# Seven products in place of eight for more of a linear attention's tiles, with the matrix's summed parts kept in memory

## The chip, the cores and the metric

The kernel runs on one core of one Trainium2 chip. The metric is the device time of one launch in microseconds, as the median of several runs; the profile is that of one more execution. Five engines matter: TensorE (PE, with its weight loads as PEld), VectorE (DVE), ScalarE (ACT), GpSimd (POOL) and SyncE (SP, which here only issues DMAs).

## The reference

A block of 2048 tokens of width 512 gets, in parallel, a linear attention with 32 heads of 16 and an MLP of 1376 hidden units with squared relu. All is float32.

```
xn  = layernorm(x)
q, k, v = split(xn @ wqkv)            # 512 x 1536
pq, pk  = phi(q), phi(k)              # phi(t) = (t > 0 ? t + 1 : exp(t)) + 1e-6
kv  = sum over tokens of pk^T v       # per head
z   = sum over tokens of pk
att = (pq @ kv) / (pq . z + 1e-6)     # per head
mlp = relu(xn @ w1 + b1)^2 @ w2 + b2
out = x + att @ wo + mlp
```

## The kernel before

**Number format and products.** Each float32 operand is held as a high and a low part (`split`: ScalarE copies to the high part, VectorE subtracts it to get the low part, called the rest), and each product is three matmuls, high by high, high by low, low by high (`PASSES`, L127). Moving operands are 512 columns wide, or 256 in the seven products.

**Order of the work.** All order is written by hand: each engine runs its instructions in the order in which the code issues them. First the kernel normalises, projects the keys and sums keys by tokens, for all 16 tiles of 128 tokens (to about 100 us). Then `kv`, block by block, is multiplied into `wo`: the result is one 512x512 matrix M (`matrix`, L948), so that attention is `q' @ M`, where q' is phi(q) divided by its denominator.

Then come two passes, n = 0 and 1, of two blocks each (a block is four tiles, 512 tokens): blocks t1 = 3 and t2 = 2 in pass 0, blocks 1 and 0 in pass 1. A pass starts with rounds p = 0 to 7 (L1171). In a round the columns `fa`, `fb` of the first weights are multiplied with both blocks at once, by seven products in place of eight (Strassen's scheme in Winograd's form). "w" rounds make hidden units of the MLP, "q" rounds queries; the order is q, w, q, w, w, w, w, and round 7 only finishes round 6. From round 4 on a round is on TensorE: A A11 and B A12 (12 matmuls), C S1 (6), the A22 product of the round before into its own bank (6), an MLP sum (12), A S2 (6), C S4 (6), a second MLP sum (12), A S3 (6).

Around that stand, in the code's order, these instructions of the other engines:

- L1184, VectorE, start of the round: reads the bank of the round before, ahead of the A22 product which goes on in that bank. Behind it stand on ScalarE a relu (L1190) and the copy of bank A (L1206).
- L1210, VectorE: adds bank B to that copy; then a relu of it (L1212).
- `hidden_2` (L457): square and high part on ScalarE, low part `s` on VectorE, once for each half of the hidden units; the MLP sums read `s`.
- `chunk_split`, `chunk_sums`, `last_split`: the next round's weights and their sums.
- L1311, VectorE: reads bank C after C S4; the next round's C S1 starts that bank anew. Then a relu (L1317).

**Steps.** The queries' way from raw q to q' is a list of steps per 128 columns (`steps_of`, L421): phi (two halves on ScalarE, L417 and L418, the last part on VectorE, L419), `weighted` (ScalarE, pz, L433), `sums` (VectorE, L438 and L439), `quotients` (L444 to L446), `divide` (L449) and, for block t1, `into_parts`. How many steps stand at which of a round's nine places says the table `AT`, for the part behind the rounds `AE`. A call of `step` takes the next of t1's list, or of t2's when t1's is empty.

**Attention.** `add_attention` (L517) adds one tile the plain way, 12 matmuls of 128x512. `Seven` (L972) does pairs of tiles r, r + 2 by seven products: it sums the four quarters of q' in place (`sums_o`), splits those sums into `so` (`parts_o`, with highs and lows), and has the same for M: sums (`sums_m`), and splits into `mt`. `run` is one product of 6 matmuls of 128x256, `into` adds a bank into the residual `res` (VectorE, L1036). In before, block 3 and block 2 are done the plain way, block 1 wholly by sevens, and block 0 by sevens for tiles 0 and 2 only. M goes raw to memory in pass 0 (`md`, L962), comes back in round 6 of pass 1, and VectorE and ScalarE sum and split it there. `matrix_parts` (L964) splits M itself for the plain way, in rounds 3 (one part), 4 (one) and 5 (two).

**Places shared in turn.** `mt` takes the place of the columns `xs0`, `so` that of `xs1`; raw M stands in the two places x0 and x1, which the residual's loads (`load_res`, L1134) take next. `add_bias` (L1143) adds b2 to the residual by accumulating DMAs on POOL.

## Time and profile before

| | |
|---|---|
| median of 3 runs (lowest, highest) | 408.36 us (408.32, 408.89) |
| the profiled execution: its time | 408.15 us |
| its span on the core | 406.4 us |
| mean granted clock of TensorE | 0.999 |
| matmuls | 1993 |

The span runs from the first to the last event of the core; the profiled execution's time holds 1.75 us more around it. In the rows of the profile an instruction stands with its start, its duration, engine, line, operation, and `out<-in` with the shape; in square brackets is the idle time of its engine before it and what ended it. Matmuls overlap: what one costs is the distance to the next one's start, not its duration. In the table of stages a row gives the stretch, its length, for each engine the busy time and the number of instructions, the granted clock, the share of the DMA engines and GB/s.

### The profile page before, as it was taken

How to read it: one execution, taken by the hardware profiler on the slowest of the kernel's cores; microseconds unless marked ns; L12 is line 12 of the kernel's file. 1: busy time of each engine (PE TensorE's matmuls, PEld its weight loads, DVE VectorE, ACT ScalarE, POOL GpSimd, SP SyncE). 2: the span in 40 equal slices, each digit the busy share in tenths (PEclk: the TensorE clock that was granted, in tenths of full speed). 3: DMA queues.
4: the chain of work that ended last, by engine and by line, in shares of the span. 5: the costliest groups of instructions: out<-in, count | busy, mean ns of one | idle time of the engine just before them, and what ended most of it. 6: DMA issues, size and time to landing. Idle time of an engine off the chain costs nothing.

```text
span 406.4 us, 5813 instructions
## 1 busy us (share of the span) xinstructions
PE 401.5 (99%) x1993; PEld 333.1 (82%) x1993; DVE 326.7 (80%) x598; ACT 274.0 (67%) x478; POOL 49.7 (12%) x81
## 2 busy tenths in 40 slices
PE   8999999999999999999999999999999999999996
PEld 7788888888788888888878888888888888888885
DVE  5886667587898999988349997567989688999885
ACT  5677777556888788886818751677587859848440
POOL 5443333220000000030000300000000200000300
PEclk9999999999999999999999999999999999999999
DMA  5856657910563231381564912412221856015612
GB/s 213 278 168 223 208 158 205 257 29 0 130 184 80 77 103 27 105 214 19 202 232 131 209 33 101 118 53 52 52 79 32 229 103 232 2 52 202 110 26 103
DMA packets 47550, 51.10 MB, mean 126 GB/s; under 512 B 8417, under 2 KB 31201, under 8 KB 47138
## 3 DMA queue, kind: packets, MB, share of 16 engines
q1 hardware_dynamic: 45138, 46.55, 37.0%
q0 software_dynamic: 2304, 4.20, 6.4%
q8 instruction: 15, 0.25, 0.2%
q14 instruction: 13, 0.11, 0.1%
q10 hardware_dynamic: 80, 0.00, 0.0%
HBM read 38.81 MB, written 10.75 MB: 122 GB/s over the span
## 4 chain that ended last, share of the span: by engine, by line
PE 97%; DMA 1%; DVE 1%; ACT 0%; issue 0%
PE acc L133 33%; PE b L497 33%; PE pk L378 11%; PE kx L398 11%; PE acc L508 2%; PE acc L1028 2%; PE pz L133 1%; PE x L1028 1%; DMA x<-in_A_x_dram 1%; PE b L133 1%; PE pz0b L133 1%; PE xh L1028 1%; PE y L1028 0%; PE acc L515 0%; PE pt L310 0%; DVE st L236 0%
## 5 line engine op out<-in xcount | busy, mean ns | idle before, releaser
L133 PE MATMUL acc<-w2r,s 128*128 128x512 f32 x477 | 113.0, 390 | 0.0
L133 PEld LDWEIGHTS acc<-w2r,s 128*128 128x128 f32 x477 | 89.2, 188 | 19.1 <-issue 0.7
L497 PE MATMUL b<-T,aop 128*128 128x512 f32 x336 | 83.5, 389 | 0.0
L497 PEld LDWEIGHTS b<-T,aop 128*128 128x128 f32 x336 | 63.0, 188 | 13.9 <-ACT t L114 0.8
L1147 POOL DMA_DIRECT2D res<-in_B_b_dram x16 | 14.4, 1042 | 277.8 <-DVE dt L439 91.0
L398 PE MATMUL kx<-pk,tok 128*128 128x512 f32 x192 | 46.0, 389 | 0.0
L398 PEld LDWEIGHTS kx<-pk,tok 128*128 128x128 f32 x192 | 36.0, 188 | 7.6 <-ACT pk L114 0.2
L497 PE MATMUL b<-xs0h,aop 128*128 128x512 f32 x112 | 36.9, 390 | 0.0
L114 ACT ACTIVATE aop<-S 128x512 fp32r<-128x512 f32 x28 | 17.5, 624 | 12.5 <-DVE S L735 12.5
L359 POOL TENSOR_TENSOR tok<-xp,tok 128x512 fp32r<-128x512 f32 x15 | 20.2, 1344 | 39.7 <-ACT tok L114 39.7
L497 PEld LDWEIGHTS b<-xs0h,aop 128*128 128x128 f32 x112 | 21.0, 188 | 4.4
L125 DVE TENSOR_TENSOR w2r<-r,w2r 128x512 fp32r<-128x512 f32 (+2 forms) x35 | 23.7, 681 | 0.5 <-ACT w2r L114 0.4
L114 ACT ACTIVATE w2r<-r 128x512 fp32r<-128x512 f32 x32 | 19.6, 619 | 6.4 <-PE acc L133 5.5
L122 DVE TENSOR_TENSOR aop<-S,aop 128x512 fp32r<-128x512 f32 x28 | 19.2, 687 | 4.8 <-ACT aop L114 4.4
L497 PE MATMUL b<-xs0l,aop 128*128 128x512 f32 x56 | 21.8, 389 | 0.0
L133 PE MATMUL acc<-mh,aTsr 128*128 128x512 f32 x64 | 20.7, 389 | 0.0
L122 DVE TENSOR_TENSOR s<-c,s 128x512 fp32r<-128x512 f32 x20 | 13.5, 688 | 8.7 <-ACT s L114 8.6
L497 PE MATMUL b<-xs1h,aop 128*128 128x512 f32 x56 | 19.5, 389 | 0.0
L114 ACT ACTIVATE T<-Tf 128x512 fp32r<-128x512 f32 x16 | 9.5, 624 | 14.4 <-DVE Tf L678 14.3
L114 ACT ACTIVATE c<-b 128x512 f32<-128x512 f32 x28 | 16.4, 587 | 2.6 <-PE b L497 2.4
L369 ACT ACTIVATE k<-pk 128x512 f32<-128x512 f32 x16 | 9.4, 590 | 9.9 <-PE pk L378 9.8
L114 ACT ACTIVATE pk<-k 128x512 fp32r<-128x512 f32 x16 | 10.1, 631 | 8.6 <-DVE k L373 8.5
(259 smaller groups left out, 828.3 us busy)
## 6 DMA issues: line engine op xcount, KB each, us to landing
r<-in_B_w_dram SPq DMA_DIRECT2D x49, 256.0 KB, 3.5
res<-in_A_x_dram SPq DMA_DIRECT2D x8, 512.0 KB, 4.7
res<-in_B_b_dram POOLq DMA_DIRECT2D x16, 256.0 KB, 5.8
out_dram<-res SPq DMA_DIRECT2D x15, 256.0 KB, 2.2
via<-xp SPq DMA_DIRECT2D x5, 512.0 KB, 2.8
xg<-via SPq DMA_DIRECT2D x20, 128.0 KB, 2.8
xTd<-t SPq DMA_DIRECT2D x8, 256.0 KB, 4.1
x<-in_A_x_dram SPq DMA_DIRECT2D x4, 512.0 KB, 4.1
```

Of the source, the lines that this page charges most:

```text
L114: nc.scalar.activation(o, i, AF.Copy, bias=bias)
L122: ENG[el].tensor_tensor(out=l, in0=src, in1=f32(h), op=OP.subtract)
L125: nc.vector.tensor_tensor(out=l, in0=src, in1=f32(h), op=OP.subtract)
L133: nc.tensor.matmul(ps, lhsT=a[u], rhs=b[v], start=first and n == 0, stop=last and n == 2)
L359: ENG[el].tensor_tensor(out=l, in0=src, in1=f32(h), op=OP.subtract)
L369: nc.scalar.activation(p, ps, AF.Relu, scale=-1.0)
L378: nc.tensor.matmul(ps, lhsT=cols(i)[u][:, j, slot(i)], rhs=w[v][:, j, :], start=first and n == 0, stop=last and n == len(steps) - 1)
L398: nc.tensor.matmul(kxp[c], lhsT=tok[i][:, u, c * P:(c + 1) * P], rhs=pk[i][:, v], start=i == 0 and (u, v) == first, stop=i == NT - 1 and ( ...
L497: nc.tensor.matmul(ps, lhsT=a[u][:, j * P:(j + 1) * P], rhs=b[v][:, j, :], start=first and j == 0 and n == 0, stop=last and j == 1 and n == 2,
L508: nc.tensor.matmul(ps, lhsT=s[u][:, k * P:(k + 1) * P], rhs=w2s[NF - 1][u][:, a:z], start=first and u == 0, stop=stop and u == 1)
L1028: nc.tensor.matmul(ps, lhsT=a, rhs=b, start=first and i == 0 and n == 0, stop=False, skip_group_check=True)
L1147: nc.gpsimd.dma_start(r[:, i], b2[None, :].partition_broadcast(P), accum_op=OP.add)
```

## The change

- In pass 0, tiles 0 and 2 of block 3 (the pass's first block) get attention by seven products, tiles 1 and 3 the plain way (`seven_half`). Block 3's q' is summed and split for that in round 6 and behind the rounds; block 2 stays plain.
- In pass 1, all four tiles of block 0 go by seven products; the MLP sum of one chunk of hidden units is kept back to stand behind them.
- The matrix's sums are made once, in pass 0: four subtractions in round 4, four splits in round 5 (`matrix_sums`, placed by the table `TM`), written to memory as high and low parts by eight DMAs of POOL. `load_m` reads both parts into `mt` in round 6 of each pass by two DMAs of POOL. The raw matrix isn't written any more, and `sums_m` and `parts_m` are gone from pass 1.
- `matrix_parts` moves to rounds 2 (one) and 3 (three).
- The steps are placed anew: the last four rows of pass 0's `AT`, the last two of pass 1's, with `step(2)` and `step(4)` behind the rounds of pass 0 and `step(4)` behind those of pass 1.

```diff
     def matrix_copy(j, ps):
...
-        nc.sync.dma_start(md[:, j], mraw[j // 2][:, j % 2])
...
+    def matrix_sums():
+
+        def op(o, x, y):
+            return lambda: nc.vector.tensor_tensor(out=o, in0=x, in1=y, op=OP.subtract)
+
+        def parts(r, at):
+            x, to = mraw[r][:, :, at], slice(2 * r, 2 * r + 2)
+            h = work.tile([P, 512], F32R, name=f"mh{r}{at.start}", tag="p", bufs=6).rearrange("p (j n) -> p j n", j=2)
+            copy("act", h, x)
+            rest_of(x.bitcast(F32R), x, h)
+            nc.gpsimd.dma_start(mtd[0][:, to, at], f32(h))
+            nc.gpsimd.dma_start(mtd[1][:, to, at], x)
+
+        (b11, b12), (b21, b22) = ([t[:, :, at] for at in (LO, HI)] for t in mraw)
+        return [op(b11, b12, b11), op(b12, b22, b12), op(b22, b22, b11), op(b21, b21, b22),
+                *(lambda r=r, at=at: parts(r, at) for r, at in ((0, LO), (0, HI), (1, HI), (1, LO)))]
...
         def load_m(self):
+
             self.mt = both("mt", ("xs0h", "xs0l"))
-            self.raw = four("mraw", "B0", pool=keep)
-            nc.sync.dma_start(self.raw, md)
-            self.m = [[self.raw[:, 2 * r:2 * r + 2, c] for c in (LO, HI)] for r in range(2)]
+            for o, src in zip(self.mt, mtd):
+                nc.gpsimd.dma_start(f32(o), src)
...
-               (3, 0, 1, 1, 0, 0, 0, 0, 0),
-               (3, 0, 0, 1, 1, 0, 1, 0, 0),
-               (1, 1, 0, 1, 1, 1, 2, 0, 1),
-               (2, 1, 4, 1, 2, 1, 0, 2, 4)),
+               (3, 0, 1, 0, 0, 0, 0, 0, 0),
+               (3, 0, 0, 1, 0, 0, 0, 0, 0),
+               (1, 1, 0, 1, 1, 1, 0, 1, 1),
+               (0, 0, 0, 0, 0, 0, 0, 0, 0)),
...
-               (1, 0, 1, 0, 0, 0, 2, 0, 0),
-               (1, 0, 1, 0, 1, 1, 0, 2, 3)))[n]
+               (1, 0, 3, 0, 0, 0, 2, 0, 2),
+               (0, 0, 0, 0, 0, 0, 0, 4, 0)))[n]
...
+        TM = {(4, 3): 1, (4, 4): 1, (4, 5): 1, (4, 6): 1,
+              (5, 1): 1, (5, 2): 1, (5, 4): 1, (5, 5): 1} if n == 0 else {}
...
-            for j in {3: (0,), 4: (1,), 5: (2, 3)}.get(p, ()) if n == 0 else ():
+            for j in {2: (0,), 3: (1, 2, 3)}.get(p, ()) if n == 0 else ():
                 matrix_parts(j)
...
+        def seven_half(half, acc, soon, later):
+
+            xh, yh = (bank(f"{w}h{half.t}")[:, LO] for w in "xy")
+            half.run(xh, ("a", 0, 0), ("m", 0, LO), 0, True)
+            half.run(acc[0][:, LO], ("a", 1, 0), ("m", 1, LO), 0)
+            half.run(acc[2][:, LO], ("a", 1, 1), ("t", 1, LO), 0)
+            half.into(xh, 0, LO)
...
-            add_attention(acc, t1 * TB)
-            wait_for(waiting[0])
-            for k in range(1, TB):
-                add_attention(acc, t1 * TB + k)
...
+            add_attention(acc, t1 * TB + 1)
+            seven_half(seven, acc, lambda: wait_for(waiting[0]), lambda: lqs.append(square_last()))
+            add_attention(acc, t1 * TB + last)
+            wait_for(waiting[1])
+            step(4)
+            xsb[:] = [both(f"xsn{k}", (f"xs{k}h", f"xs{k}l")) for k in range(2)]
...
-            mlp_2(acc, f, s.pop(f))
+            if n == 0 or e < NF - 3:
+                mlp_2(acc, f, s.pop(f))
...
-            add_attention(acc, t2 * TB + 1)
-            add_attention(acc, t2 * TB + last, True)
...
+            f = waiting[-3]
+            s3 = s.pop(f)
+            for k in (last, *range(last)):
+                three(acc[k], [s3[:, u, k * P:(k + 1) * P] for u in range(2)], w2s[f], False, k == last)
```

## The prediction

> **What bounds the kernel now.** I read the busy times first, then TensorE's waits, then a table of the stages the change touches, then those stages engine by engine. Round p of pass n is named n.p, as above.

> ```profile
> PE 401.5 (99%) x1993; PEld 333.1 (82%) x1993; DVE 326.7 (80%) x598; ACT 274.0 (67%) x478; POOL 49.7 (12%) x81
> ...
> PE warm L528 <- PEq L1546: 0.8, 1, 0.8
> PE pt L310 <- DVE xp L600: 0.4, 1, 0.4
> ...
> 147.60:162.50 14.90, 14.90 (x67) 12.35 (x66) 13.47 (x26) 12.85 (x23) 0.00 (x0) 1.00 0.25 71
> 162.50:177.50 15.00, 15.00 (x68) 12.39 (x68) 14.21 (x27) 12.31 (x22) 2.17 (x3) 1.00 0.49 159
> 177.50:192.50 15.00, 15.00 (x68) 12.43 (x67) 12.44 (x22) 11.48 (x19) 1.60 (x2) 1.00 0.39 70
> ```

> TensorE waits twice, both times in the first microseconds, and never again: the time is its list of matmuls. Two things follow. Fewer matmuls are worth their full issue time, and each new wait of TensorE is lost in full. The table (columns: sum, PE, PEld, DVE, ACT, POOL, clock, DMA share, GB/s) gives rounds 0.4, 0.5 and 0.6: VectorE is busy 13.47 of 14.90 us, 14.21 of 15.00 and 12.44 of 15.00. It has 1.4, 0.8 and 2.6 us to spare, in pieces that stand where it waits for ScalarE or TensorE.

> **What the change takes from TensorE.** The end of before holds both ways side by side.

> ```profile
> 387.50 0.28 PE L1028 MATMUL xh<-mh,aTsr 128*128 128x256 f32 x1
> ...
> 389.65 0.39 PE L133 MATMUL acc<-mh,aTsr 128*128 128x512 f32 x1
> ...
> 395.11 0.29 PE L1028 MATMUL acc<-mh,so0h 128*128 128x256 f32 x1
> ...
> 398.11 0.86 PE L133 MATMUL acc<-w2r,s 128*128 128x512 f32 x3
> ```

> Between these starts lie 18, then 24 matmuls of 128x256 for two tiles by seven products (2.15 + 3.00 = 5.15 us), and 24 of 128x512 for two tiles the plain way (5.46 us): 0.1226 and 0.2275 us each. Two tiles change sides in block 3 and two in block 0. The saving is 2 x 0.31 = 0.62 us. [...]

> **What it adds beside TensorE.** In pass 0: one of the matrix splits moves to round 2, three stand in round 3 where one stood; four subtractions come into round 4 and four splits with eight DMAs into round 5; sums and splits for half of block 3 come into round 6 and after. Four steps leave rounds 4 to 6 and two leave round 7, for later. In pass 1 the matrix's sums and splits vanish, and ten steps come earlier. On engines with spare time this would be free; but each adds to a queue in order, so I carry the queue forward from row to row. The order of a round is that of the section above.

> ```profile
> 130.83 0.69 DVE L122 TENSOR_TENSOR s<-c,s 128x512 fp32r<-128x512 f32 x1 [1.14 <-ACT s L114]
> ...
> 148.94 0.69 DVE L1311 TENSOR_TENSOR c<-b,c 128x512 f32<-128x512 f32 x1
> ...
> 170.56 1.28 DVE L122 TENSOR_TENSOR ml<-m,mh 128x512 fp32r<-128x512 f32 x2
> ...
> 150.28 2.88 PE L497 MATMUL b<-T,aop 128*128 128x512 f32 x12
> ```

> **Wait 1, start of C S1 in 0.4.** Two VectorE operations take 1.28 us, 0.60 apart. Round 2's one falls mostly into the 1.14 us gap; ScalarE's copy ahead of it leaves 0.14. Round 3's two add 1.20. So L1311 of round 3 goes from 148.94 to 150.3 and ends at 150.98. It reads bank C, which C S1 overwrites at 150.28. TensorE waits 0.75, after 0.05 from end to start.

> ```profile
> 149.66 0.72 ACT L485 ACTIVATE r2b<-c,b1s 128x512 f32<-128x512 f32 x1 [1.07 <-DVE c L1311]
> ...
> 152.74 0.69 DVE L1210 TENSOR_TENSOR c<-b,c 128x512 f32<-128x512 f32 x1 [0.40 <-ACT c L114]
> ...
> 163.98 0.68 DVE L1184 TENSOR_TENSOR t<-b,t 128x512 f32<-128x512 f32 x1
> ...
> 165.26 2.88 PE L497 MATMUL b<-T,aop 128*128 128x512 f32 x12
> ```

> **Wait 2, A22 product in 0.5.** L1311 releases ScalarE's chain, which ends in L1210, so L1210 moves as much, by 1.33, to 154.07. From it to L1184 of round 5 VectorE works 11.24 us without a gap worth naming; now a split less and four subtractions more, +1.8: L1184 at 167.1, ended 167.8. The A22 product that overwrites its bank stands six matmuls after 165.26, with wait 1 at 167.37: 0.49.

> ```profile
> 159.08 0.80 ACT L433 ACTIVATE pz<-q,zc 128x512 f32<-128x512 f32 x1
> ...
> 164.69 0.73 ACT L485 ACTIVATE r2b<-t,b1s 128x512 f32<-128x512 f32 x1
> ...
> 166.54 0.70 DVE L438 STREAM_TRANSPOSE pt<-pz 128x512 f32<-128x512 f32 x1
> ...
> 169.35 0.69 DVE L449 SCALAR_TENSOR_TENSOR q<-q,pz 128x512 f32<-128x512 f32 x1
> ...
> 167.98 2.88 PE L133 MATMUL acc<-w2r,s 128*128 128x512 f32 x12
> ...
> 173.42 2.88 PE L133 MATMUL acc<-w2r,s 128*128 128x512 f32 x12
> ```

> **Wait 3, second MLP sum in 0.5.** From L1184's end ScalarE does relu (0.61) and the copy of the bank (0.58): L1210 at 169.05. In before the transpose followed at once, for its pz was made in round 4 (159.08). The pz now heads round 5's steps: relu 0.61 and pz 0.82 first, VectorE idle for 1.5 us, transpose at 171.23. Sums and quotients take 2.7 (166.54 to 169.35), a weight rest and a matrix rest 1.2: the low half of s at 175.1, ended 175.8. TensorE needs it at 174.66 + 0.45 (173.42 with 1.24 of waits, third matmul; 12 of them take 2.72 from 165.26 to 167.98, so 0.2267 each): 0.75.

> ```profile
> 168.82 1.14 ACT L114 ACTIVATE mh<-m 128x512 fp32r<-128x512 f32 x2
> ...
> 173.58 0.42 DVE L735 TENSOR_TENSOR S<-r 128x256 f32<-128x256 f32 x1
> ...
> 175.03 0.62 ACT L417 ACTIVATE phi<-q 128x512 f32<-128x512 f32 x1
> ...
> 183.92 0.63 ACT L459 ACTIVATE c<-c 128x512 f32<-128x512 f32 x1
> ...
> 184.58 0.63 ACT L114 ACTIVATE s<-c 128x512 fp32r<-128x512 f32 x1
> ...
> 388.27 1.80 DVE L986 TENSOR_TENSOR q<-q 128x256 f32<-128x256 f32 x4
> ```

> **Wait 4, A22 in 0.6.** From that s at 175.12 VectorE has 6.0 us up to L1311 of round 5: the chunk sums (1.47 from 173.58 on), one operation of 0.34 and seven of 0.60, two of them new. L1311 starts at 181.16 and ends at 181.84. The last matrix part's copy stands on ScalarE behind the relu that waits for L1311 (0.61 + 0.63, to 183.1); its rest stands on VectorE ahead of a weight rest and L1184, which so starts at 184.34 and ends at 185.02. TensorE goes on from wait 3 at 175.86, has 34 matmuls of 0.2267 up to A22, and is there at 183.57: 1.50.

> **Wait 5, second MLP sum in 0.6.** The steps of this round stand one behind the other: phi, pz, sum. So the chain from L1184 is one of round trips: relu, a copy into parts and the copy of the bank on ScalarE, L1210 on VectorE (186.9), relu and phi's two halves (0.61, 0.65, 0.65) on ScalarE, phi's last part on VectorE (189.55), then pz, relu, square (0.65) and copy (0.63) on ScalarE, and the low half of s at 193.02, ended 193.7. TensorE needs it 32 matmuls after the start of A22 (185.07), at 192.32: 1.43.

> **Wait 6, A22 in 0.7.** VectorE goes on with the other s (194.2), quotients (1.3), division, L1311 (196.7), waits for relu and phi's halves again, and does phi (199.4), the four half sums (1.80), a weight rest and L1184, ended 203.1. TensorE goes on from wait 5 at 193.75 and has 28 matmuls ahead of A22, to 200.1: 3.05. That makes 7.97 us in pass 0. What stands behind, lows and adds, finds time: VectorE idled 5 us from 204 on in before, and the steps put off fill that.

> ```profile
> 337.10 0.69 DVE L419 SCALAR_TENSOR_TENSOR q<-q,phi 128x512 f32<-128x512 f32 x1
> ...
> 343.23 2.18 ACT L114 ACTIVATE so1h<-q 128x512 fp32r<-128x512 f32 x4
> ...
> 345.79 0.65 DVE L1184 TENSOR_TENSOR t<-b,t 128x512 f32<-128x512 f32 x1
> ...
> 348.00 1.53 PE L497 MATMUL b<-T,aop 128*128 128x512 f32 x6
> ```

> **Waits 7 and 8, pass 1.** From phi at 337.10 VectorE in round 1.6 now does transpose and sum ahead of s (which stays in time by 0.1), then quotients, division and the next phi, so that L1311 moves from 341.88 (in before ahead of all these) to 344.6. ScalarE's relu and the four highs (2.18) follow, and only then the pz of the next step, at 348.0; VectorE's transpose and sum wait for that pz, and L1184 stands behind them: 350.26 in place of 345.79, ended 350.95. TensorE wants to start A22 at 348.00: 2.95. Four more steps stand on VectorE between the seven products, where four lows stood, 3.9 us against 2.4; the adds out of xs come some 0.5 later than TensorE needs its bank again.

> **The end.** Block 0 by sevens in full has ten adds into the residual instead of five.

> ```profile
> 396.76 0.42 DVE L1036 TENSOR_TENSOR res<-xh,res 128x256 f32<-128x256 f32 x1 [0.86 <-PE xh L1028]
> ```

> Some five more at 0.42, so 2.1 us. They stand beside the 12 matmuls of the MLP sum that is kept back to the end (12 x 0.2275 = 2.7 us), and the last two adds and stores are as before: nothing. Without that cover it would be up to 2 us.

> **DMA.** Eight writes of 256 KB in place of four, four loads of 1 MB in place of one.

> ```profile
> md<-m SPq DMA_DIRECT2D x4, 256.0 KB, 2.9
> ...
> mraw<-md SPq DMA_DIRECT2D x1, 1024.0 KB, 4.9
> ...
> res<-in_A_x_dram SPq DMA_DIRECT2D x8, 512.0 KB, 4.7
> ...
> res<-in_B_b_dram POOLq DMA_DIRECT2D x16, 256.0 KB, 5.8
> ```

> They move from SP to POOL, which issues one in about 1 us (2.17 us for the three in 0.5 that the table counts) and is else idle. The last part (183.8) is written by 187.6, the two loads behind it have landed by 197.4 and are read at 208.7. The residual's load shares its place with the raw matrix and waits with SP's queue until 187.6; load and bias are done by about 202, first used at 208. Without the waits everything stands 8 us earlier. I cost this at nothing; without the cover it would be the rival below.

> **Sum.** 0.75 + 0.49 + 0.75 + 1.50 + 1.43 + 3.05 + 2.95 + 0.50 = 11.4 us of waits, less 0.62: 408.15 (the profiled execution; span 406.4, 0.2 below the median of the runs) + 10.8 = 419.0.

> **Rivals.** *Some of the waits only.* A queue that TensorE's own wait lets catch up need not be late again; waits 1 to 3 come of plain work, half of 7 too: 3.5 - 0.6 gives 411.0 (409 to 414). For it: the round trips are worth nothing if ScalarE runs ahead. *Enough idle time: faster.* Up to A22 of 0.7 VectorE gains eight matrix operations and four half sums (8 x 0.60 + 1.80 = 6.6 us) and loses the VectorE work of six steps (3.9), 2.7 net against the 4.8 us idle in the table. If the order lets it use that time, nothing waits and the time is 408.15 - 0.62 = 407.5. It decides as long as L1311 of 0.3 ends before 150.28; it has 0.66 to give there, and I add 1.3. *The transfers are late:* if the eight writes drain singly, 2.9 each from the first rest of 0.5 (174.5) on, the last has landed at 197.7 in place of 187.6, and the first add into the residual comes some 3 us after 208, with TensorE behind it: 422. *The clock drops.*

> ```profile
> 403.00:406.40 3.40, 0.00 (x0) 0.00 (x0) 0.36 (x1) 0.00 (x0) 0.00 (x0) 0.84 0.44 154
> ```

> TensorE has ended at 402.9, and the mean clock of 0.84 means half speed from about 405.3, 2.4 us later; nowhere else does it idle so long. Waits 6 and 7 are longer. No row shows how long it stays down: nothing, or, taking as long as the fall, 2.4 us at half speed each, +2.4: 421.4. [...]

> **Chances.** All waits, 0.54 (own range 414 to 420.5); some, 0.22; faster, 0.08; late transfers, 0.04; clock, 0.12. Range 410.5 to 422.5: it leaves out the faster case, a quarter of the second and the far ends above. Faster by over 0.2% (0.8 us, about what a measurement of this kernel can tell): 0.08; within: 0.02, the low end of the second; slower: 0.90.

> **What would show it.** TensorE's list of waits names L1311 in 0.4, L1184 in 0.5, 0.6, 0.7 and 1.7, and s in 0.5 and 0.6, with about these times; pz stands directly ahead of the transposes. A list as empty as before's proves me wrong on all of it, and so does an L1311 of 0.3 that ends before C S1. If waits 1 to 3 are there and 4 to 6 not, the second case holds; if matmuls behind a wait stand 0.45 us apart, the last.

## The result, and the profile after

The changed kernel takes 423.35 us (median of 5, 423.18 to 424.98), against 408.32 us for before (median of 5): 1.0376 times the time, with an interval of 1.0356 to 1.0396. The profiled execution took 424.05 us, its span is 422.0 us. The forecast was 419.0 us with 422.5 as the upper end: the direction is right, the size too small by 4.35 us, and the time lies outside the range.

The page of the changed kernel, busy times:

```profile
PE 407.3 (97%) x2029; PEld 336.6 (80%) x2029; DVE 334.9 (79%) x616; ACT 276.0 (65%) x482; POOL 57.4 (14%) x93
```

TensorE does 36 matmuls more, smaller ones, and is busy 5.8 us longer; VectorE has 8.2 us of work more, ScalarE 2.0. TensorE's waits in the changed kernel (engine, tile and line, what it waited for, us in total, times, longest):

```profile
PE b L497 <- DVE t L1197: 8.3, 3, 4.4
PE acc L133 <- ACT s L114: 0.9, 1, 0.9
PE warm L528 <- PEq L1590: 0.8, 1, 0.8
PE acc L133 <- DVE s L122: 0.5, 1, 0.5
PE pt L310 <- DVE xp L600: 0.3, 1, 0.3
PE b L497 <- ACT c L114: 0.3, 1, 0.3
```

L1197 is what L1184 was in before, the read of a bank ahead of the A22 product. Where before had no wait behind the start, there are six now (the three at L1197 are listed in one line), five of them at places that the forecast named. The timeline of TensorE in the changed kernel, with the idle time ahead of a group in brackets:

```profile
146.36 1.65 PE L497 MATMUL b<-T,aop 128*128 128x512 f32 x6 [0.26 <-ACT c L114]
...
175.49 2.60 PE L133 MATMUL acc<-w2r,s 128*128 128x512 f32 x10 [0.47 <-DVE s L122]
...
184.70 1.66 PE L497 MATMUL b<-T,aop 128*128 128x512 f32 x6 [1.17 <-DVE t L1197]
...
192.72 3.29 PE L133 MATMUL acc<-w2r,s 128*128 128x512 f32 x12 [0.92 <-ACT s L114]
...
204.50 2.93 PE L497 MATMUL b<-T,aop 128*128 128x512 f32 x6 [4.41 <-DVE t L1197]
...
362.67 2.10 PE L497 MATMUL b<-T,aop 128*128 128x512 f32 x6 [2.68 <-DVE t L1197]
```

The bracket holds a little less than what a wait costs, 4.41 us for 4.57 at wait 6 and 2.68 for 2.84 at wait 7, because matmuls overlap: the one at 210.85 takes 0.39 us, and the next starts 0.23 later. The full cost is how much later the next group starts than the same group of before, so I went through the starts from one wait to the next. All measured terms are those of the one profiled execution, which took 0.7 us more than the median; over the five executions the mean clock goes from 0.987 to 0.991, so the half clock need not be equally long in each.

| term | forecast, us | measured, us |
|---|---|---|
| wait 1, rounds 0.3 and 0.4 | 0.75 | 0.80 |
| wait 2, A22 in 0.5 | 0.49 | 0.43 |
| wait 3, second MLP sum in 0.5 | 0.75 | 0.80 |
| wait 4, A22 in 0.6 | 1.50 | 1.48 |
| wait 5, second MLP sum in 0.6 | 1.43 | 1.49 |
| wait 6, A22 in 0.7 | 3.05 | 4.57 |
| wait 7, A22 in 1.7 | 2.95 | 2.84 |
| wait 8 | 0.50 | 0 |
| half clock behind wait 6 | 0 | 2.72 |
| half clock behind wait 7 | 0 | 1.65 |
| seven products | -0.62 | -0.86 (0.30 + 0.56) |
| sum | 10.8 | 15.9 |

The spans differ by 15.6 us; of the rest, 0.25 us is an earlier start of the profiled execution. The measured sum is 5.1 us above the forecast's. Two terms make more than that, 1.5 us more in wait 6 and 4.4 us of half clock; the missing wait 8 and the larger saving take back 0.7 us.

**Wait 6.** VectorE's timeline of the changed kernel ahead of it:

```profile
196.45 0.68 DVE L1319 TENSOR_TENSOR c<-b,c 128x512 f32<-128x512 f32 x1
200.84 0.69 DVE L419 SCALAR_TENSOR_TENSOR q<-q,phi 128x512 f32<-128x512 f32 x1 [3.71 <-ACT phi L418]
```

L1319 (L1311 of before) starts at 196.45; 196.7 was forecast. Then VectorE waits for ScalarE, as forecast, but until 200.84 and not 199.4. What ScalarE and SyncE do at that time, from the timeline of all engines:

```profile
187.32 0.38 SPq L1146 DMA_DIRECT2D res<-in_A_x_dram  x1
187.81 0.40 SPq L167 DMA_DIRECT2D r<-in_B_w_dram  x1
...
198.38 0.63 ACT L114 ACTIVATE w2r<-r 128x512 fp32r<-128x512 f32 x1 [4.04 <-DMA r<-in_B_w_dram]
```

The residual's two loads hold SyncE's queue for 7.94 us, from 179.76 on, until GpSimd has written the matrix away, because they share the matrix's place; the second is the first row above. Behind it in that queue stands the load of a piece of the second MLP matrix, issued only at 187.81. Its data reach ScalarE at 198.4, and the relu and phi's halves stand behind that copy.

**The clock.** Stretches of the changed kernel behind waits 6 and 7, from the table of stages (stretch, length, busy time and instructions of PE, PEld, DVE, ACT, POOL, granted clock, DMA share, GB/s):

```profile
202.00:204.00 2.00, 0.00 (x0) 0.00 (x0) 1.93 (x5) 0.66 (x3) 0.00 (x0) 0.81 0.16 29
...
206.00:208.00 2.00, 2.00 (x6) 1.60 (x5) 0.00 (x0) 0.53 (x1) 0.00 (x0) 0.50 0.00 0
...
210.00:212.00 2.00, 2.00 (x12) 1.75 (x12) 0.92 (x2) 1.94 (x5) 0.00 (x0) 0.98 1.02 426
...
362.00:364.00 2.00, 1.33 (x5) 1.14 (x6) 1.90 (x6) 1.32 (x3) 0.00 (x0) 0.92 0.00 0
```

A mean of 0.81 over 2 us is 0.76 us at half, so the fall is at 203.24; by the same sum the rise is at 210.08. That is 6.84 us at half clock, of which TensorE worked 5.58, from 204.50 on; half of that is 2.79 us, and the starts give 2.72. The last row gives the fall behind wait 7: a mean of 0.92 is 0.32 us at half, so it is at 363.68.

### The profile page after: what moved, and what is told of

It is laid out like the page before. It is cut to its first block, busy times and chain, and to the rows that moved or that the text cites. A ratio compares the mean times of both kernels' runs of the same rounds, so it can differ in the third digit from the quotient of the medians.

```text
span 422.0 us, 5924 instructions
## 1 busy us (share of the span) xinstructions
PE 407.3 (97%) x2029; PEld 336.6 (80%) x2029; DVE 334.9 (79%) x616; ACT 276.0 (65%) x482; POOL 57.4 (14%) x93
## 4 chain that ended last, share of the span: by engine, by line
PE 73%; DVE 15%; ACT 6%; DMA 3%; issue 3%; SPq 0%; DVEq 0%; ACTq 0%
PE acc L133 21%; PE b L497 19%; PE pk L378 10%; PE kx L398 10%; PE acc L1034 3%; DMA r<-in_B_w_dram 2%; DVE aop L122 2%; PE acc L508 2%; DVE S L735 1%; PE pz L133 1%; PE x L1034 1%; PE xl L1034 1%; DVE w2r L125 1%; ACT r2a L485 1%; DVE s L122 1%
## 5 line engine op out<-in xcount | busy, mean ns | idle before, releaser
L133 PE MATMUL acc<-w2r,s 128*128 128x512 f32 x477 | 113.8, 391 | 1.4 <-ACT s L114 0.9
L133 PEld LDWEIGHTS acc<-w2r,s 128*128 128x128 f32 x477 | 89.0, 188 | 21.8 <-DVE s L122 1.5
L497 PE MATMUL b<-T,aop 128*128 128x512 f32 x336 | 86.3, 398 | 8.7 <-DVE t L1197 8.3
L497 PEld LDWEIGHTS b<-T,aop 128*128 128x128 f32 x336 | 63.4, 191 | 25.0 <-DVE t L1197 10.1
L114 ACT ACTIVATE aop<-S 128x512 fp32r<-128x512 f32 x28 | 17.5, 624 | 14.3 <-DVE S L735 14.3
L114 ACT ACTIVATE w2r<-r 128x512 fp32r<-128x512 f32 x32 | 19.6, 621 | 10.8 <-PE acc L133 5.9
L122 DVE TENSOR_TENSOR aop<-S,aop 128x512 fp32r<-128x512 f32 x28 | 19.2, 686 | 3.9 <-ACT aop L114 3.6
L433 ACT ACTIVATE pz<-q,zc 128x512 f32<-128x512 f32 x16 | 12.9, 806 | 8.7 <-DVE q L419 8.7
L497 PE MATMUL b<-xs0h,aop 128*128 128x512 f32 x56 | 18.5, 391 | 0.0
L497 PE MATMUL b<-xsn0h,aop 128*128 128x512 f32 x56 | 18.4, 389 | 0.0
L438 DVE STREAM_TRANSPOSE pt<-pz 128x512 f32<-128x512 f32 x16 | 11.3, 705 | 8.3 <-ACT pz L433 8.3
L114 ACT ACTIVATE c<-b 128x512 f32<-128x512 f32 x28 | 16.4, 586 | 2.3 <-PE b L497 2.0
L122 DVE TENSOR_TENSOR s<-c,s 128x512 fp32r<-128x512 f32 x20 | 13.4, 688 | 4.9 <-ACT s L114 4.9
L114 ACT ACTIVATE pk<-k 128x512 fp32r<-128x512 f32 x16 | 10.1, 630 | 8.0 <-DVE k L373 8.0
L1008 POOL DMA_DIRECT2D mth<-mthd x2 | 1.1, 568 | 103.1 <-DVE aop L122 102.2
L386 DVE SCALAR_TENSOR_TENSOR pk<-k,pk 128x512 fp32r<-128x512 f32 x16 | 11.3, 708 | 4.6 <-ACT pk L114 2.7
## 6 DMA issues: line engine op xcount, KB each, us to landing
r<-in_B_w_dram SPq DMA_DIRECT2D x49, 256.0 KB, 3.1
res<-in_A_x_dram SPq DMA_DIRECT2D x8, 512.0 KB, 4.7
res<-in_B_b_dram POOLq DMA_DIRECT2D x16, 256.0 KB, 6.9
out_dram<-res SPq DMA_DIRECT2D x15, 256.0 KB, 2.2
via<-xp SPq DMA_DIRECT2D x5, 512.0 KB, 2.6
xTd<-t SPq DMA_DIRECT2D x8, 256.0 KB, 3.4
x<-in_A_x_dram SPq DMA_DIRECT2D x4, 512.0 KB, 3.9
```

The costliest lines, as they stand in the source:

```text
L114: nc.scalar.activation(o, i, AF.Copy, bias=bias)
L122: ENG[el].tensor_tensor(out=l, in0=src, in1=f32(h), op=OP.subtract)
L133: nc.tensor.matmul(ps, lhsT=a[u], rhs=b[v], start=first and n == 0, stop=last and n == 2)
L386: nc.vector.scalar_tensor_tensor(pk[i][:, 1], p, 1e-6, f32(pk[i][:, 0]), op0=OP.add, op1=OP.subtract)
L433: nc.scalar.activation(pz, o, AF.Identity, bias=zc[:, 1, j:j + 1], scale=zc[:, 0, j:j + 1])
L497: nc.tensor.matmul(ps, lhsT=a[u][:, j * P:(j + 1) * P], rhs=b[v][:, j, :], start=first and j == 0 and n == 0, stop=last and j == 1 and n == 2,
```

## The experiments

Three questions: do the waits come of the order of the steps or of the amount of work on VectorE and ScalarE; is wait 6's surplus the queue; and what sets the clock. Then: is there a version that keeps the gain.

**Second pass's steps as in before.** The edit, as in the next three on the changed kernel:

```diff
-               (1, 0, 3, 0, 0, 0, 2, 0, 2),
-               (0, 0, 0, 0, 0, 0, 0, 4, 0)))[n]
+               (1, 0, 1, 0, 0, 0, 2, 0, 0),
+               (0, 0, 0, 0, 0, 0, 0, 2, 0)))[n]
```

> The changed kernel (423.35 us) with pass 1's steps placed as before the change. Theory (the order of the steps makes the wait ahead of the A22 product in round 1.7, 2.84 us, and the half clock behind it costs 1.65 us more): both go, 418.9 us, TensorE waits for nothing in pass 1. Rival (the larger loads of the summed matrix and the kept-back sum make pass 1 late, whatever the steps): the wait stays, 423 us. A third outcome, 420.5 us, would say that the clock falls in pass 1 without that wait.

Measured: 425.62 us (424.70 to 426.16), 1.0421 times before [1.0401, 1.0440]. TensorE's waits in this run:

```profile
PE b L497 <- DVE t L1197: 4.7, 2, 3.5
PE xl L1034 <- DVE res L1042: 2.8, 1, 2.8
PE acc L133 <- DVE w2r L125: 1.7, 1, 1.7
```

Wait 7 is gone (two waits at L1197, both in pass 0), so it came of the steps pulled forward. But 4.7 us come back at the end, and the time is above all three cases of the expectation. TensorE waits there for a rest of the second MLP matrix (1.7 us), for an add into the residual (2.8) and for a low part (0.2), all late on VectorE, where the steps put off now stand; and the clock is at half behind the 2.8: from 406.3 to 411.9 the matmuls of 128x256 start 0.21 us apart, ahead of that wait and from 412.1 on 0.12. Putting the steps back where before had them gains nothing here.

**Residual's load a round later.**

```diff
-            if p == NO - 3 + 1 - n:
+            if p == (NO - 3 if n else NO - 1):
                 load_res(t1)
```

> The changed kernel with pass 0's residual load issued one round later, so that SP's queue isn't held by it and the weight piece behind it comes in time. Theory (1.5 us of the wait in round 0.7 is a ScalarE copy that waited 4 us for that weight piece): the wait falls from 4.57 to about 3.1 us, the time to 421.9 us if the clock still falls for as long, to about 420 us if it falls for one window less, 419.2 us if it stays up. Rival (the transfer is late but VectorE's and ScalarE's chains alone set the wait): no change, 423.3 us.

Measured: 421.69 us (420.09 to 421.75), 1.0318 [1.0298, 1.0338]. TensorE's timeline of this run at wait 6:

```profile
203.20 1.88 PE L497 MATMUL b<-T,aop 128*128 128x512 f32 x6 [2.66 <-DVE t L1197]
```

The wait falls from 4.41 to 2.66 us of idle time with only that load moved, so the surplus was the queue. The other waits stay. In this run's profiled execution the clock is at half for 3.42 us behind wait 6, from 204.46 to 207.88, and not for 6.84; it took 2.3 us less than the profiled execution of the changed kernel. The wait varies from execution to execution: in the run with the second pass's steps as in before, whose pass 0 is unchanged, wait 6 was 3.48 us.

**First pass's steps as in before**, the matrix's work as changed:

```diff
-               (3, 0, 1, 0, 0, 0, 0, 0, 0),
-               (3, 0, 0, 1, 0, 0, 0, 0, 0),
-               (1, 1, 0, 1, 1, 1, 0, 1, 1),
-               (0, 0, 0, 0, 0, 0, 0, 0, 0)),
+               (3, 0, 1, 1, 0, 0, 0, 0, 0),
+               (3, 0, 0, 1, 1, 0, 1, 0, 0),
+               (1, 1, 0, 1, 1, 1, 2, 0, 1),
+               (0, 0, 0, 0, 0, 0, 0, 2, 0)),
```

> The changed kernel with pass 0's steps of rounds 4 to 7 placed as before the change, the matrix's work where the change put it. Theory A (round trips of steps that stand one directly behind the other make the waits of rounds 5 to 7): pass 0's waits fall from 9.6 to 5 or 6 us, 418 to 419 us. Theory B (the amount of VectorE's work ahead of the A22 product of round 7 makes them): 3.9 us of steps come back into those rounds, the waits rise to 11 us or more, 425 us or more.

Measured: 421.28 us (421.11 to 421.64), 1.0318 [1.0303, 1.0334]. The time lies between the two cases of the expectation. Waits 3 and 5 are gone; the A22 waits stay, 1.51 us of idle time in 0.6 and 4.24 in 0.7. So the order of the steps makes the waits at the MLP sums (pz late, as forecast). The 4.24 us in 0.7 are not the same wait as before the edit, though:

```profile
198.74 0.63 ACT L114 ACTIVATE w2r<-r 128x512 fp32r<-128x512 f32 x1 [5.18 <-DMA r<-in_B_w_dram]
...
199.41 0.69 DVE L125 TENSOR_TENSOR w2r<-r,w2r 128x512 fp32r<-128x512 f32 x1 [2.66 <-ACT w2r L114]
```

VectorE, shortly ahead of the read that A22 waits for, stands idle for 2.66 us until the late piece is there. So in this order up to 2.66 of the 4.24 us are the queue's; what would be left without it was not run.

**Without the matrix's subtractions and splits.**

```diff
-            return lambda: nc.vector.tensor_tensor(out=o, in0=x, in1=y, op=OP.subtract)
+            return lambda: None
...
-            copy("act", h, x)
-            rest_of(x.bitcast(F32R), x, h)
-            nc.gpsimd.dma_start(mtd[0][:, to, at], f32(h))
+            nc.gpsimd.dma_start(mtd[0][:, to, at], x)
```

> The changed kernel without the matrix's subtractions and splits in pass 0: the raw matrix goes to memory in place of the parts (same eight transfers), so the attention by seven products computes with a wrong matrix. 4.8 us of VectorE's and 2.1 us of ScalarE's work are gone from rounds 4 and 5; the steps stay as the change has them. Theory A (round trips of the steps): waits 3, 5 and 6 stay for the most part, pass 0's waits 9.6 to about 6 us, 419 us. Theory B (amount of work): waits 2 to 6 go to under 2 us in all and the clock stays up in pass 0, 412 to 414 us (pass 1's 4.5 us and round 3's 0.8 us stay).

Measured: 414.39 us (414.17 to 414.86), 1.0150 [1.0135, 1.0165]. In the first pass only 0.25 us and 1.37 us of idle time are left, the latter at A22 in 0.7, and no half clock there: the execution's mean of 0.996 is what the 3.41 us at half behind wait 7 make; wait 7 stays at 2.68. So 9.0 of the 15.0 us go with eight VectorE and four ScalarE operations (8 x 0.60 + 4 x 0.55, so 7 us of work), and with the clock in the first pass. But the edit frees the queue as well, since the raw matrix is written away earlier and its place comes free:

```profile
173.00 0.94 SPq L1143 DMA_DIRECT2D res<-in_A_x_dram  x2
```

The residual's load holds SyncE for 0.94 us and not for 7.94. The queue alone was worth 1.7 us in the run with the load a round later; the rest, by estimate 7 us, goes to the work and to the clock that its waits cost. That is more than the 2.1 us that the order of the first pass's steps was worth. The parts overlap, and no run tells them apart fully.

**Forced waits in before.** A chain of GpSimd subtractions writes the low half of one MLP tile's input again in pass 0, with four, five and seven of them (k below), and TensorE waits for the last:

```diff
         for e, f in enumerate(waiting[:-2]):
+            if (n, e) == (0, 4):
+                for _ in range(k):
+                    nc.gpsimd.tensor_tensor(out=s[f][:, 1], in0=r2[f], in1=f32(s[f][:, 0]), op=OP.subtract)
             mlp_2(acc, f, s.pop(f))
```

> Kernel: before, with five subtractions of 128x512 on GpSimd that rewrite the low half of one MLP tile's input in the first pass, so that TensorE has to wait once for it, by estimate 2.2 us. Theory (TensorE's clock is set by the idle time within a window of 3.41 us, of which a part is enough): the time is before's plus the wait, 410.5 us, and 1.7 us more (412.2) if the wait falls into one window and 2 us of it is enough. Rival (only a window idle from end to end lowers the clock): 410.5 us and the clock stays at 1.00 behind the wait.

> Kernel: as the run with the short gap, with seven subtractions, so that the wait is by estimate 4.9 us. Theory (part of a window is enough): 413.3 us plus 1.7 us for each window of 3.41 us at half clock, one or two of them, 415 to 416.7 us; the half clock shows within 3.5 us after the gap's start or end. Rival (a whole window must be idle): 4.9 us contain a whole window only if they begin in its last or first 1.5 us, so one window at most, 413.3 or 415 us.

> Kernel: as the run with five subtractions, with four, which by the two waits measured (3.79 us for five, 6.79 for seven, so 1.50 us each) makes a wait of 2.3 us. Theory (about 2 us of idle time in a window of 3.41 us are enough): if the wait falls into one window, the next one is at half clock, 408.4 + 2.3 + 1.7 = 412.4 us; if the grid cuts it in two parts of under 1.5 us, 410.7. Rival (a whole window must be idle): 410.7 us and full clock.

Measured, one execution each: 410.90 us with a wait of 2.11 us and full clock; 413.65 with 3.79 us, then half clock for 3.42 us; 417.17 with 6.79 us, then half clock for 6.84 us. The waits are longer than estimated for five and seven, but the sums hold: 408.5 + 3.8 + 1.7 = 414.0 and 408.5 + 6.8 + 1.7 + 0.3 = 417.3 (0.3 for the 0.57 us of work in the first 3.41 us at half). The wait of 2.11 us decides nothing: where the grid found below stood in that execution is not shown. The longest wait, from its table of stages:

```profile
226.00:228.00 2.00, 0.00 (x0) 0.00 (x0) 2.00 (x2) 0.00 (x0) 1.84 (x3) 0.64 0.62 110
...
232.00:234.00 2.00, 2.00 (x7) 1.53 (x7) 1.97 (x4) 1.97 (x5) 0.00 (x0) 0.65 0.87 154
```

The fall is at 226.56, the rise at 233.40, 6.84 us or twice 3.42 later. TensorE was idle from 222.61 to 229.40. So the window from 226.56 to 229.97, idle for 2.84 us and not from end to end, kept the clock down in this run. The five-subtraction run can't tell the theories apart either, since its wait filled a whole window. The finer answer comes from runs made for another purpose. The run without the matrix's work, at its wait in pass 1 (idle from 350.48 to 353.16):

```profile
354.00:354.50 0.50, 0.50 (x4) 0.41 (x3) 0.47 (x2) 0.47 (x2) 0.00 (x0) 1.00 0.00 0
354.50:355.00 0.50, 0.50 (x4) 0.46 (x3) 0.50 (x1) 0.50 (x1) 0.00 (x0) 0.65 0.00 0
358.00:358.50 0.50, 0.50 (x6) 0.50 (x5) 0.18 (x1) 0.50 (x2) 0.00 (x0) 0.94 0.00 0
```

Half clock from 354.65 to 358.06, 3.41 us; the 3.41 us before hold 1.92 us of idle time. And the run with the first pass's steps as in before, at wait 6 (idle from 198.47 to 202.70):

```profile
200.00:200.50 0.50, 0.00 (x0) 0.00 (x0) 0.47 (x3) 0.50 (x2) 0.00 (x0) 1.00 0.35 53
202.50:203.00 0.50, 0.30 (x1) 0.30 (x2) 0.15 (x1) 0.32 (x1) 0.00 (x0) 1.00 0.03 4
203.50:204.00 0.50, 0.50 (x3) 0.39 (x2) 0.00 (x0) 0.47 (x2) 0.00 (x0) 0.60 0.00 0
```

The fall is at 203.60, so by the grid found below a window ended 3.41 us earlier, at 200.19. The window up to there held 1.72 us of idle time, and the clock stayed at 1.00; the next held 2.51, and it fell.

**The last block alone, the matrix's work on GpSimd.** Block 3 is plain again; the eight operations of the matrix, and the low halves of its plain split, go to GpSimd, which is idle there. The edit on the changed kernel, its core:

```diff
-            return lambda: nc.vector.tensor_tensor(out=o, in0=x, in1=y, op=OP.subtract)
+            return lambda: nc.gpsimd.tensor_tensor(out=o, in0=x, in1=y, op=OP.subtract)
...
-            rest_of(x.bitcast(F32R), x, h)
+            nc.gpsimd.tensor_tensor(out=x.bitcast(F32R), in0=x, in1=f32(h), op=OP.subtract)
...
-               (1, 0, 3, 0, 0, 0, 2, 0, 2),
-               (0, 0, 0, 0, 0, 0, 0, 4, 0)))[n]
+               (1, 0, 3, 0, 0, 0, 0, 0, 2),
+               (0, 0, 0, 0, 0, 0, 0, 1, 0)))[n]
...
             wait_for(waiting[1])
+            step(5)
```

> Kernel: the first pair's first block is plain again as in before; the last block stays seven products; the matrix's sums, rests and low halves are kept in memory as changed, but GpSimd makes them, in rounds 0.5 and 0.6, and the second pass asks VectorE for one step instead of four at its last place and five steps after the second wait of the second part. Theory (the time was lost to the amount of VectorE's and ScalarE's work ahead of the sums that TensorE waits for, and to the clock that these waits cost): no wait of over 1 us at the second sum of the attention in either pass, no lower clock, and the end keeps its gain of about 0.56 us, so 407.4 to 408.0 us. Rival (the five late steps come too late for the four seven-product tiles, as in the run with the second pass's steps as in before): 1 to 3 us of waits near the end, 409 to 411 us, more if the clock falls. Rival (GpSimd's work slows VectorE or the late memory copies hold a queue): the wait at the attention's second sum in round 0.7 stays at 1.4 us or more, 409 to 413 us.

Measured: 418.90 us (418.35 to 419.90), 1.0248 [1.0227, 1.0268]. Wait 7 is gone, but VectorE's read of bank C (L1318 here, L1311 in before) is late for C S1 in 0.6 by 2.94 us, and the clock is at 0.50 from 184.34 to 191.17, 6.83 us:

```profile
184.97 5.46 PE L497 MATMUL b<-T,aop 128*128 128x512 f32 x12 [2.94 <-DVE c L1318]
```

VectorE's timeline of this run, and GpSimd's:

```profile
171.65 1.79 DVE L125 TENSOR_TENSOR w2r<-r,w2r 128x512 fp32r<-128x512 f32 x1
173.37 3.48 DVE L122 TENSOR_TENSOR s<-c,s 128x512 fp32r<-128x512 f32 x2
...
178.47 1.51 DVE L735 TENSOR_TENSOR S<-r 128x256 f32<-128x256 f32 x1
...
182.01 0.68 DVE L122 TENSOR_TENSOR aTsr<-q,aTsr 128x512 fp32r<-128x512 f32 x1
```

```profile
171.18 3.42 POOL L122 TENSOR_TENSOR ml<-m,mh 128x512 fp32r<-128x512 f32 x2 [12.60 <-ACT mh L114]
174.56 1.74 POOL L974 TENSOR_TENSOR m<-m 128x512 f32<-128x512 f32 x1
176.38 3.32 POOL L974 TENSOR_TENSOR m<-m,m 128x512 f32<-128x512 f32 x2
179.78 1.35 POOL L974 TENSOR_TENSOR m<-m 128x512 f32<-128x512 f32 x1
```

As long as GpSimd works, from 171.2 to 181.1, a VectorE subtraction of 128x512 takes 1.79 us, and one of 128x256 1.51 in place of 0.42 in before's row; when GpSimd is done it takes 0.68 again. Of the expectation, the third case's reason holds (GpSimd's work slows VectorE), but not its place, A22 in 0.7, nor its range of 409 to 413 us: in these rows GpSimd's spare time is not spare for VectorE.

**Both blocks, the matrix's work on GpSimd**, with the plain tiles of block 3 ahead of the seven products and the parts read back later:

```diff
             add_attention(acc, t1 * TB + 1)
-            seven_half(seven, acc, lambda: wait_for(waiting[0]), lambda: lqs.append(square_last()))
             add_attention(acc, t1 * TB + last)
+            seven_half(seven, acc, lambda: wait_for(waiting[0]), lambda: lqs.append(square_last()))
```

> Kernel: the whole change, with both tiles of seven products, but the matrix's sums, rests and low halves are made by GpSimd in rounds 0.5 and 0.6 instead of VectorE, the summed matrix is read back one round later, the residual's load comes two rounds later, the steps of the first pass stand as in before but for two, and both plain tiles run ahead of the seven products. Theory (amount of VectorE's and ScalarE's work): VectorE still has the half tile's own sums in the first pass, but none of the matrix's, so waits of 0 to 2 us in the first pass, gain 0.86 us, and 407.5 to 409.5 us with no lower clock, up to 412 with one. Rival (the seven products' own sums are what makes VectorE late): wait of 2 us or more at the attention's second sum in round 0.7 and a lower clock behind it, 411 to 415 us.

Measured: 431.61 us (431.34 to 432.20), 1.0564 [1.0543, 1.0586], the slowest of all and beyond both ranges. To the wait in 0.6 (2.97 us) come one in 0.7 (3.66), 4.9 us at the adds out of the seven products of block 3, 0.9 for the parts read back, and a mean clock of 0.976. The run doesn't separate the seven products' own sums from what GpSimd's work does to VectorE.

**The last block alone, the matrix's work in VectorE's idle time.** In before VectorE idles 1.98, 2.79 and 5.13 us behind round 0.7 and ScalarE 8.46. The matrix is stored whole as in before and read back in round 0.6 into the place of two operand tiles that are free until the next pass. The edit on the kernel with the last block alone, its core:

```diff
+        raw, high = four("mraw", "B0", pool=keep), []
+        nc.sync.dma_start(raw, md)
...
+        else:
+            do(m_sums, 4)
         s1 = hidden_2(f"s{n}_{f}", c21)
...
                 if k == 2:
                     lqs.append(square_last())
+                    do(m_sums, 4)
+                    T.update({t: tokens_sum(t, f"B{t - 1}") for t in (1, 2)})
```

> Kernel: as the run with the first block plain (the last block alone gets seven products for all four tiles), but nothing of the matrix's work is on GpSimd or in the rounds: the matrix is stored whole as in before, read back in round 0.6, and VectorE and ScalarE make its sums, highs and rests behind round 0.7, where the trace of before shows VectorE idle for 1.98, 2.79 and 5.13 us and ScalarE for 8.46 us. In the second pass the third wait comes ahead of the five late steps, and the last block's four high halves come behind two copies of the second MLP matrix. Theory (what counts is the amount of work ahead of a sum that TensorE waits for, and VectorE is slower while GpSimd works): no wait over 0.3 us and no lower clock, so before's 408.4 us less the end's 0.56: 407.6 to 408.2 us. Rival (the end's four tiles want their sums earlier than VectorE can give them, wherever the matrix's work stands): 0.5 to 2 us of waits in the last 30 us, 408.3 to 410 us. Rival (the read and the two stores of the matrix hold the MLP's pieces or the residual): a wait of 1 us or more between rounds 0.6 and the first pass's adds, 409 us or more.

Measured: 411.11 us (410.83 to 411.73), 1.0065 [1.0047, 1.0082]. No wait in any round, none over 0.7 us behind the start, the mean clock is 0.999; but the time is 2.9 us above before, outside the theory's range, and the waits lie between 226 and 234 us. What is left is one hand-over; ScalarE's timeline of this run:

```profile
219.62 0.63 ACT L114 ACTIVATE T<-Tf 128x512 fp32r<-128x512 f32 x1 [11.41 <-DMA mtld<-mraw]
```

ScalarE's first copy for the next pass goes into the place that the matrix's last store is still reading, and all that ScalarE has behind it comes late for the MLP pieces.

**That copy three places later**, and three late steps for five:

```diff
-            do(prepare, (1, 0, 0, 1, 0, 2, 2, 3, 1, 3, 1)[e])
+            do(prepare, (0, 0, 0, 2, 0, 2, 2, 3, 1, 3, 1)[e])
...
-            step(5)
+            step(3)
```

> Kernel: as the run with the sums in idle time, but the first copy into the operand tile that shares its memory with the matrix stands three places later (in the trace of that run ScalarE waits 11.41 us there for the matrix's last store to memory, and TensorE stands still for 1.5 us and more in the 15 us behind it), and three steps instead of five stand behind the third wait of the second pass. Theory (that copy is all that is left): the 2.8 us that TensorE loses between 217 and 235 us go, and the end keeps 0.1 to 0.56 us of its gain: 407.7 to 408.3 us. Rival (the stores themselves hold the MLP's pieces, whichever copy waits): the waits for pieces of the second MLP matrix near 226 and 232 us stay, 409.5 to 411 us.

Measured: 409.34 us (409.12 to 411.37), 1.0030 [1.0018, 1.0042]. The loss behind 217 us is gone, so it was the copy and not the stores; but the time is neither theory's, for a wait of 1.26 us stands at 378.65, where the run before had one of 0.17. The second edit is the only one of the two that changes the second pass:

```profile
PE acc L133 <- DVE w2r L125: 1.3, 1, 1.3
```

**That wait taken away**, by VectorE's order alone:

```diff
             wait_for(waiting[2])
-            step(3)
+            wait_for(waiting[3])
+            step(5)
...
-              (3, 2, 2, 3, 0, 5, 1, 6, 1, 5, 0))[n]
+              (1, 2, 2, 3, 0, 5, 1, 6, 1, 5, 0))[n]
```

> Kernel: as the run with the tile later, but in the second pass the fourth wait, too, comes ahead of the late steps, which are five again, and only one step instead of three follows the next MLP sum. The run with the tile later has one wait left, 1.26 us at 378 us for a piece of the second MLP matrix whose rest VectorE makes behind three steps. Theory (nothing but VectorE's order at that place is late): the 1.26 us go, so 408.3 less 0.1 to 0.56: 407.7 to 408.2 us. Rival (VectorE has too little time there for the steps of four tiles in any order): a wait of 0.3 to 1.3 us at another place of the last 40 us, 408.4 to 409.6 us.

Measured: 407.63 us (407.28 to 408.13), against 408.12 for the runs of before beside it: 0.9988 times before [0.9978, 0.9997], so 0.49 us less (0.1 to 0.9 by the interval). The page of this run and its list of waits:

```profile
PE 400.9 (99%) x2011; PEld 333.6 (82%) x2011; DVE 330.5 (81%) x603; ACT 274.4 (68%) x478; POOL 56.6 (14%) x91
```

```profile
PE warm L528 <- PEq L1592: 0.8, 1, 0.8
PE pt L310 <- DVE xp L600: 0.3, 1, 0.3
```

TensorE waits where before's does, at the start, and nowhere else. The end of the changed kernel saves 0.56 us, and the 0.49 agree with it. The half of the change that made block 3's two tiles go by seven products isn't in it: its 0.30 us were not tried in such an order.

## Why the prediction was right and wrong

- **What bounds the kernel, and the cost of a wait.** Right: every idle time of TensorE came back in full, 12.4 us in the table's waits, and before's empty list of waits is what a good version has, too.
- **The saving.** 0.62 forecast, 0.86 measured. What is left over is at the end, 0.56 for 0.31: there the 84 small matmuls of block 0 take 10.03 us, 0.1194 each, where the forecast had 0.1226.
- **Waits 1 to 5 and 7.** 7.87 us forecast, 7.84 measured; no single one is off by more than 0.11. Carrying each queue forward from row to row gave the sizes, and the places but for wait 1 and in part wait 5. Of wait 1 about half stands ahead of A S3 in round 0.3, where ScalarE's copy of the bank comes behind three matrix copies (0.41); of the rest only 0.15 us stand at C S1, where all 0.75 were forecast, and 0.13 and 0.11 in the groups around it. That wait 1's total fits is luck. Of wait 5, 1.08 us are for ScalarE's high part of s; the forecast named the low part alone. The reason that the forecast named for wait 3 and wait 5, a pz made too late, is shown by the run with the first pass's steps as in before. That for 7 is shown by the run with the second pass's.
- **Wait 8.** 0.50 forecast, absent: VectorE's adds end at 374.8, TensorE needs the bank at 375.6. The half clock behind wait 7 had put TensorE back by 1.65 us by then; whether the wait would stand without it is not shown.
- **DMA.** "I cost this at nothing" is the first step that failed. I had put the residual's load behind the matrix's writes and asked when the residual was needed. I had not asked what stood behind that load on SyncE's queue. A piece of the MLP matrix did, and it cost 1.5 us in wait 6; the run with the load a round later shows it.
- **The clock.** The second step that failed, and the larger one: the sum took nothing for it, the rival had 2.4 us and a chance of 0.12, and it cost 4.4 us. A row that hinted at it was quoted: half speed 2.4 us after TensorE's end. From it I took the time to the fall for the time below. By these stretches of 6.84 and 3.41 us, three windows of 3.41 us at half would by estimate have been up to 1.7 us each, 5.1 us on top of 419.0, and a range drawn around that would have held the time. By these sizes one of the two errors alone would have left the time below 422.5: 423.35 less 1.5 or less 4.4 us is 421.8 or 419.0.
- **The rivals.** Waits 1 to 3 and 7 stayed, and so did 4 to 6, so "some of the waits" fell. "Late transfers" had the wrong victim, the residual and not the piece behind it. "Enough idle time" was wrong for this order. The last run's 407.63 us are near that rival's 407.5 by chance: it does half of the change, with the matrix's work at another place. What it shows is that for this half there is an order in which nothing waits.

## What to carry to other kernels

Work added to an engine that is 80% busy is free only where it idles; carry its queue forward from row to row, and look for the place where both helpers idle at once. For each transfer that has to wait, ask first what stands behind it on its queue. Here the eleven waits of the table below, of 2.66 to 6.79 us, also cost half the clock for 3.41 to 6.84 us, so in this kernel price such a wait at its length plus, by estimate, 1.7 us for each 3.41 us at half; another kernel was not run.

## What the runs showed of the hardware

Eleven stretches with a granted clock of 0.50 stand in the tables of stages of eight executions. The last two columns give the idle time of TensorE in the 3.41 us ahead of the fall and in the 3.41 us behind it.

| run | wait, us | fall | rise | at 0.50, us | idle ahead, us | idle behind, us |
|---|---|---|---|---|---|---|
| the changed kernel, wait 6 | 4.41 | 203.24 | 210.08 | 6.84 | 3.15 | 1.26 |
| the same, wait 7 | 2.68 | 363.68 | 367.09 | 3.41 | 2.40 | 0 |
| second pass's steps as in before, wait 6 | 3.48 | 203.84 | 207.25 | 3.41 | 3.27 | 0 |
| residual's load a round later, wait 6 | 2.66 | 204.46 | 207.88 | 3.42 | 2.15 | 0 |
| the same, wait 7 | 2.72 | 361.48 | 364.89 | 3.41 | 2.31 | 0 |
| first pass's steps as in before, wait 6 | 4.24 | 203.60 | 207.01 | 3.41 | 2.51 | 0 |
| the same, wait 7 | 2.68 | 360.61 | 364.02 | 3.41 | 2.68 | 0 |
| without the matrix's work, wait 7 | 2.68 | 354.65 | 358.06 | 3.41 | 1.92 | 0 |
| last block alone, matrix on GpSimd, C S1 in 0.6 | 2.94 | 184.34 | 191.17 | 6.83 | 2.31 | 0.63 |
| five subtractions in before | 3.79 | 226.15 | 229.57 | 3.42 | 3.41 | 0.05 |
| seven subtractions in before | 6.79 | 226.56 | 233.40 | 6.84 | 3.41 | 2.84 |

By that grid the clock fell behind windows with 1.92 us of idle time and more, and did not behind the one with 1.72 in the run with the first pass's steps as in before. The wait of 2.11 us, with four subtractions, left it at 1.00; but the grid can cut a wait in two, so these lengths are no bounds by themselves. The clock came back after windows with 0 to 0.05 us of idle time; those with 0.63, 1.26 and 2.84 were followed by another at 0.50. So a wait of 2.94 us brought 6.83 us at half clock.

In the run with the last block alone and the matrix's work on GpSimd, subtractions on VectorE and on GpSimd at the same time took longer: those of 128x512 on VectorE 1.74 to 1.79 us (0.68 behind GpSimd's end), and on GpSimd 1.66 to 1.74 in the rows from 171.18 to 176.38. A GpSimd subtraction of the same size at 190.46, with VectorE operations of one input beside it (L444 to L446), took 1.34, and they took 0.17, 0.35 and 0.71 us, in before 0.17, 0.35 and 0.72. Which of the two is served first was not tried.
